# Joining low weight bits by OR, splitting early value products by query tile, and padding TensorE waits with identity products

## The chip, the cores and the metric

The kernel runs on one core of one Trainium2 chip. The metric is device time in microseconds (us) of one launch; lower is better. A core has five engines that run side by side and meet through semaphores: TensorE (PE; its weight loads are listed as PEld), VectorE (DVE), ScalarE (ACT), GpSimd (POOL) and SyncE (SP), which here only issues DMAs.

## The reference

Attention with a mask from a hash, and then a two-layer block on its output, all in float32:

```
q_bits = (q @ proj > 0);  k_bits = (k @ proj > 0)            # 6 bits, bucket = the number they form
mask   = q_bucket[:, :, :, None] == k_bucket[:, :, None, :]
scores = where(mask, q @ k.T / 8, -1e9)                      # B, H, S, D = 4, 8, 768, 64
attn   = softmax(scores)
x      = (attn @ v) as rows of 3072 tokens x 512
h      = x @ w_in                                            # 512 x 2048
out    = (s * relu(h)**2 + b) @ w_out                        # 2048 x 512
```

The inputs q, k, v and both weight matrices come in as 8-byte floats, which the kernel reads as pairs of 32-bit words.

## The kernel before

**Tiling and stages.** There are 32 visits (4 batches x 8 heads). A visit has 3 slots, each of 256 queries (two query tiles of 128, `TPC` = 2), so 96 slots in all. For each slot `weights` (L593 on) makes scores on TensorE (L608, L609), a row maximum on VectorE (L613), the exponential on ScalarE (L614) and the normalization on GpSimd (L633). `values` (L649 on) then multiplies by the values. The 16 token groups of the two-layer block follow in `moe`: first layer on TensorE (L776 to L778), square and scale on ScalarE and GpSimd (L786 to L790), second layer on TensorE (L803). Work of `moe` starts as soon as a batch is complete and is mixed with the attention of the next batches.

**Early and late.** The first ten visits (`FULL` = 10, 30 slots) take the early way: the normalized weights are transposed on TensorE (L665), copied out of PSUM by ScalarE or VectorE (the helper `copy`, L228), and multiplied with the values in plain float32 (L672), three steps a slot. A step has two products: key tile m = 0 goes into rows 0 to 63 of PSUM bank 4, key tile m = 1 into rows 64 to 127, both for all 256 queries. `finish` then adds the two halves: a scaled copy of the upper one (L719, ScalarE or VectorE), and a multiply-add of the lower one on VectorE (L720). Later visits use float16 pairs (L678, L684) and end in the same `finish`.

**Weight decoding.** 32 tiles of 128 x 512 weights (16 of w_in, 16 of w_out) are decoded in `decode` while the attention runs. For each, ScalarE rescales the high word (L382, into `osb`) and takes the top three bits of the low word as a number (L383). VectorE isolates the sign (L384), then shifts the high part left by three and puts the sign back (L385). GpSimd adds the three low bits as an integer (L389 for w_out, L395 for w_in). Then the value is split into a high and a low part.

**The order.** Nothing is issued in program order. Every step is entered in a `Plan` with an engine, a cost that is expected for it, what it reads and writes, and a priority. `Plan.order` (L73) is a list scheduler: it gives each step a start time by these costs, may choose between engines for a step with several ways, and emits all steps in order of start. Each engine executes its own steps in that order. In the plan, TensorE steps that start before `WARM` = 30 cost 1.7 times as much. So a changed cost anywhere changes the order of all that comes after.

**Start.** Ten products of the identity with itself (L298, float32, 128 x 128) are issued to TensorE before the plan begins. A float32 product is two records in the trace.

Of the kernel before, what the change touches and what calls it, by code (L numbers as in the profile page):

```python
# [33 lines left out]
class Plan:  # L34
# [3 lines left out]
    def __init__(self):  # L38
        self.steps = []
        self.writer = {}  # L40
        self.readers = {}
        self.moves = set()
        self.spread = {}
        self.owners = {}

    def add(self, eng, cost, fn, r=(), w=(), pr=0.0, lag=0.0):
        self.any([(eng, cost, fn)], r, w, pr, lag)

    def any(self, ways, r=(), w=(), pr=0.0, lag=0.0):

        i = len(self.steps)
        if "all" in w or "all" in r:
            self.spread[i] = "all" in w
        if SHARED in w:
            self.owners[i] = set()
        elif SHARED in r:
            self.owners[self.writer[SHARED]].add(i)
        deps = set()
        for k in r:
            if k in self.writer:  # L60
                deps.add(self.writer[k])
            self.readers.setdefault(k, []).append(i)
        for k in w:
            if k in self.writer:
                deps.add(self.writer[k])
            deps.update(self.readers.get(k, ()))
        for k in w:
            self.writer[k] = i
            self.readers[k] = []
        deps.discard(i)  # L70
        self.steps.append((ways, pr, lag, deps))

    def order(self):  # L73
        n = len(self.steps)
        left = [len(s[3]) for s in self.steps]
        users = [[] for _ in range(n)]
        for i, s in enumerate(self.steps):
            for d in s[3]:
                users[d].append(i)
        ready = [0.0] * n  # L80
        free = {}
        moved = 0.0
        open_ = {}
        where = {}
        live, over, held = set(), 0.0, False

        def offer(i):
            for way in self.steps[i][0]:
                open_.setdefault(way[0], []).append(i)

        def best(e, t):
            found = None
            for i in open_[e]:
                if i in self.owners or self.spread.get(i):
                    ready[i] = max(ready[i], over)
                    if held or (live and i in self.spread):
                        continue
                if ready[i] > t + LOOK.get(e, 0.0):
                    continue
                ways, pr = self.steps[i][:2]  # L100
                if found is not None and found[:2] <= (pr, i):
                    continue
                if len(ways) > 1:
                    mine = max(t, ready[i]) + next(c for x, c, _ in ways if x == e) + BIAS.get(e, 0.0)
                    if any(max(free.get(x, 0.0), ready[i]) + c + BIAS.get(x, 0.0) < mine - 1e-9 for x, c, _ in ways if x != e):
                        continue
                found = (pr, i)
            return found
        for i in range(n):
            if not left[i]:  # L110
                offer(i)
        out = []
        while len(out) < n:
            times = sorted((max(free.get(e, 0.0), min(ready[i] for i in lst)), k, e) for k, (e, lst) in enumerate(open_.items()) if lst)
            for t, _, e in times:
                found = best(e, t)
                if found is not None:
                    break
            if found is None:
                continue  # L120
            i = found[1]
            ways, pr, lag, deps = self.steps[i]
            for x, _, _ in ways:
                open_[x].remove(i)
            eng, cost, fn = next(z for z in ways if z[0] == e)
            where[i] = eng
            self.steps[i] = ([(eng, cost, fn)], pr, lag, deps)
            start = max(free.get(e, 0.0), ready[i])
            if e == PE and start < WARM:
                cost *= 1.7  # L130
            free[e] = start + cost
            end = start + cost + HOP[e]
            if e == SP or i in self.moves:
                moved = max(moved, start + cost) + lag
                end = moved + HOP[SP]
            else:
                end += lag
            out.append((start, i))
            if i in self.owners:
                live |= self.owners[i]  # L140
            if i in self.spread:
                held = self.spread[i]
            if i in live or i in self.spread:
                live.discard(i)
                over = max(over, end)
            for u in users[i]:
                same = any(x == e for x, _, _ in self.steps[u][0])
                ready[u] = max(ready[u], end - (SAME[e] if same else 0.0))
                left[u] -= 1
                if not left[u]:  # L150
                    offer(u)
        self.length = max(free.values())
        self.start = {i: t for t, i in out}
        return [i for _, i in sorted(out)]

# [1 line left out]
ABIAS = 0.0  # L159
HOP = {None: 0.0, PE: 0.2, DVE: 0.13, ACT: 0.2, POOL: 0.1, SP: 2.4}  # L160
SAME = {None: 0.0, PE: 0.2, DVE: 0.0, ACT: 0.05, POOL: 0.0, SP: 0.0}
WARM = 30.0
BIAS = {DVE: DBIAS, ACT: ABIAS}
SHARED = ("b", 0)
LOOK = {PE: 0.0, DVE: 0.0, ACT: 0.1}
# [3 lines left out]
def lsh_attention_moe(ctx: ExitStack, tc, q, k, v, proj, w_in, w_out, s, b, out):  # L169
# [39 lines left out]
    def dve(n, fn, r, w, pr, ns=None):  # L209
        plan.add(DVE, ((n + 64) / 960.0 if ns is None else ns), fn, r, w, pr)  # L210

    def act(n, fn, r, w, pr, more=0.0, late_=0.0):
        plan.add(ACT, 0.21 + n / 1470.0 + more, fn, r, w, pr, late_)
# [45 lines left out]
    def late(w):  # L259
        return w >= FULL  # L260
# [97 lines left out]
    def decode(u, pr):  # L358
# [8 lines left out]
        def raw():  # L367
            return box["t"]

        def words(z):  # L370
            return box["t"].rearrange("p n t -> p (n t)")[:, z * 512:(z + 1) * 512]
# [8 lines left out]
            n, j = key[1:]  # L380
            dve(1, lambda: nc.vector.tensor_reduce(wmx[:, j:j + 1], raw()[:, :, 1].bitcast(F32), AX.X, ALU.max, apply_absolute_value=True), rk, [("wx", j)], pr, 0.65)
        act(512, lambda: nc.scalar.activation(g, raw()[:, :, 1].bitcast(F32), AF.Copy, scale=float(2.0**-112)), rk + [("pace", u % PACE)], [gk], pr)  # L382
        act(512, lambda: nc.scalar.activation(words(0), raw()[:, :, 0].bitcast(U32), AF.Copy, scale=float(2.0**-29)), [], rk, pr)  # L383
        dve(256, lambda: nc.vector.tensor_scalar(words(1), gi, -2**31, None, ALU.bitwise_and), [gk], rk, pr, 0.45)  # L384
        dve(512, lambda: nc.vector.scalar_tensor_tensor(gi, gi, 3, words(1), ALU.logical_shift_left, ALU.bitwise_or), rk, [gk], pr, 0.7)  # L385
        if not wi:
            def swap():
                wt[key] = wk.tile([P, 2, 512], F32R, tag=f"w{u}", name=f"w{u}")
            pool(512, lambda: nc.gpsimd.tensor_tensor(gi, gi, words(0), ALU.add), rk, [gk], pr)  # L389
            plan.add(None, 0.0, swap, [], rk + wk_, pr)  # L390
            copy(512, lambda: wt[key][:, 0], lambda: g, [gk], [key + (0,)], pr, (ACT, POOL))
            plan.any([(POOL, 1.4, lambda: nc.gpsimd.tensor_tensor(wt[key][:, 1], g, f32(wt[key][:, 0]), ALU.subtract)),
                      (DVE, 0.7, lambda: nc.vector.tensor_tensor(wt[key][:, 1], g, f32(wt[key][:, 0]), ALU.subtract))], [gk, key + (0,)], [key + (1,)], pr)
            return
        pool(512, lambda: nc.gpsimd.tensor_tensor(words(0), gi, words(0), ALU.add), [gk], rk, pr)  # L395
        held_raw.append((words, rk, key))
        if j < NC_ - 1:
            return
# [250 lines left out]
    def values(i, pr, pieces):  # L649
# [19 lines left out]
        def product(f):  # L669
            def mm():  # L670
                for m in range(2):
                    nc.tensor.matmul(av[m * D:(m + 1) * D], VF[x][:, 2 * f + m], PF[r][f][:, m], start=(f == 0), stop=(f == HT - 1))  # L672
            pe(FPC, mm, TK(r, f, 3) + VK(x), [("b", 4)], pr)

        def high(first=True):
# [32 lines left out]
    def finish(i, av, pr):  # L708
# [5 lines left out]
            xp[key] = xpb[:, nx[0] % NXP], ("xp", nx[0] % NXP)  # L714
            nx[0] += 1
        t, tk = xp[key]
        xh, xk = t[hh * D:(hh + 1) * D], [tk + (hh,)]
        scale = 1.0 / TOP if late(w) else 1.0
        some(CH, lambda e: e.mul(xh, av[0:D], scale) if e is nc.scalar else e.tensor_scalar(xh, av[0:D], scale, None, ALU.mult), [], xk + [("b", 4)], pr, (ACT, DVE))  # L719
        dve(CH, lambda: nc.vector.scalar_tensor_tensor(xh, av[D:P], scale, xh, ALU.mult, ALU.add), [], xk + [("b", 4)], pr, 0.45)  # L720
        if hh:

            xk = [tk + (0,), tk + (1,)]
            if late(w) != late(w - 1):
                raise ValueError("both heads of a pair in one way")
            up = vsc[:, bb, 0:1]
# [148 lines left out]
    queue = plan.order()  # L875
    with tc.manual_schedule(engines={PE, DVE, ACT, POOL, SP}):
        for i in queue:
            plan.steps[i][0][0][2]()


# [20 lines left out]
GATE = lambda KK, AK: AK(0)  # L901
FULL = 10
PASS = 2
FPC = 0.48
WP = -8
MP = 0.0
PP = 0
# [26 lines left out]
```

## Time and profile before

| | |
|---|---|
| device time, median of 3 runs | 973.07 us (972.75 to 977.53) |
| the profiled execution, its own time | 973.05 us |
| its span, first to last instruction | 971.3 us |
| TensorE busy | 927.7 us, 96% |
| mean granted TensorE clock | 0.981 of full speed |

The profiled execution is as long as the median one, and 1.75 us of its time lie outside the span. "Busy" is the time in which at least one instruction of a kind is in flight. A row of the profile's groups gives the line of the kernel, engine, operation, output<-input, shapes, the count, then busy us, mean ns of one, and the idle time of the engine right before these instructions with what ended it.

### The profile page before, as it was taken

How to read it: one execution, taken by the hardware profiler on the slowest of the kernel's cores; microseconds unless marked ns; L12 is line 12 of the kernel's file. 1: busy time of each engine (PE TensorE's matmuls, PEld its weight loads, DVE VectorE, ACT ScalarE, POOL GpSimd, SP SyncE). 2: the span in 40 equal slices, each digit the busy share in tenths (PEclk: the TensorE clock that was granted, in tenths of full speed). 3: DMA queues.
4: the chain of work that ended last, by engine and by line, in shares of the span. 5: the costliest groups of instructions: out<-in, count | busy, mean ns of one | idle time of the engine just before them, and what ended most of it. 6: DMA issues, size and time to landing. Idle time of an engine off the chain costs nothing.

```text
span 971.3 us, 17425 instructions
## 1 busy us (share of the span) xinstructions
PE 927.7 (96%) x6152; PEld 716.6 (74%) x6152; DVE 623.6 (64%) x1042; ACT 663.0 (68%) x1224; POOL 625.7 (64%) x709
## 2 busy tenths in 40 slices
PE   8998797999999999989999999999999999999998
PEld 5766564666767777857778788878787788888886
DVE  6697898888897666776666776767778764000000
ACT  3777887887877667766777677777776776434342
POOL 2456865689799856756757777776666676433333
PEclk6998999999999999989999999999999999999999
DMA  4276666555978898987798898798897875201000
GB/s 121 78 204 161 197 164 181 148 150 162 240 168 183 183 202 195 190 185 152 151 200 169 159 189 186 151 201 161 169 197 164 159 143 112 72 1 44 11 23 22
DMA packets 303719, 144.40 MB, mean 149 GB/s; under 512 B 264256, under 2 KB 286784, under 8 KB 303632
## 3 DMA queue, kind: packets, MB, share of 16 engines
q1 hardware_dynamic: 298432, 126.25, 59.9%
q10 hardware_dynamic: 5200, 17.05, 5.6%
q8 instruction: 48, 0.79, 0.3%
q14 instruction: 39, 0.32, 0.1%
HBM read 51.38 MB, written 14.16 MB: 67 GB/s over the span
## 4 chain that ended last, share of the span: by engine, by line
PE 47%; issue 3%; POOL 2%; ACT 2%; DVE 1%; POOLq 0%; DVEq 0%; ACTq 0%
PE bank L803 17%; PE bank L776 6%; PE bank L778 5%; PE bank L777 5%; PE bank L608 3%; PE bank L678 3%; PE bank L609 3%; PE bank L684 2%; POOL glb L790 1%; POOL rb L789 1%; PE bank L478 1%; PE bank L495 0%; PE bank L497 0%; PE bank L496 0%; DVE pb L641 0%
## 5 line engine op out<-in xcount | busy, mean ns | idle before, releaser
L633 POOL TENSOR_SCALAR eb<-eb,st 128x768 f32<-128x768 f32 x176 | 205.2, 1171 | 76.8 <-DVE st L624 56.5
L803 PE MATMUL bank<-w,ghb 128*128 128x512 f32 x768 | 213.4, 407 | 0.1
L613 DVE TENSOR_REDUCE st<-bank 128x1 f32<-128x768 f32 x192 | 180.3, 953 | 51.0 <-PE bank L609 43.6
L776 PE MATMUL bank<-xc,wi 128*128 128x256 f16 x768 | 211.8, 276 | 0.3 <-ACT rb L786 0.3
L777 PE MATMUL bank<-xc,wi 128*128 128x256 f16 x768 | 209.8, 273 | 0.0
L778 PE MATMUL bank<-xc,wi 128*128 128x256 f16 x768 | 209.8, 273 | 0.0
L614 ACT ACTIVATE eb<-bank,st 128x768 f32<-128x768 f32 x176 | 157.5, 895 | 72.0 <-DVE pb L641 38.0
L641 DVE SCALAR_TENSOR_TENSOR pb<-eb,pb 128x768 f16<-128x768 f32 x132 | 144.7, 1100 | 54.2 <-ACT pb L640 53.7
L789 POOL TENSOR_SCALAR rb<-rb,misc 128x512 f32<-128x512 f32 x96 | 87.4, 910 | 126.6 <-ACT ghb L788 115.4
L786 ACT ACTIVATE rb<-bank,dsc 128x512 f32<-128x512 f32 x96 | 65.9, 686 | 146.4 <-PE bank L778 130.6
L608 PE MATMUL bank<-ks,aq 128*128 128x384 f32 x384 | 148.7, 387 | 11.9 <-ACT eb L614 8.8
L803 PEld LDWEIGHTS bank<-w,ghb 128*128 128x128 f32 x768 | 135.7, 189 | 22.5 <-issue 0.8
L790 POOL TENSOR_TENSOR glb<-rb,ghb 128x512 fp32r<-128x512 f32 x96 | 130.8, 1363 | 5.3
L609 PE MATMUL bank<-ks,bq 76*128 76x384 f32 x384 | 133.9, 349 | 0.0
L640 ACT ACTIVATE pb<-eb 128x768 f16<-128x768 f32 x132 | 110.1, 836 | 12.8 <-DMA tb<-pb 9.8
L803 PE MATMUL bank<-w,glb 128*128 128x512 f32 x384 | 110.9, 400 | 2.1 <-POOL glb L790 1.3
L776 PEld LDWEIGHTS <-wi 128*128 128x128 f16 x768 | 75.1, 98 | 46.4 <-issue 39.2
L608 PEld LDWEIGHTS bank<-ks,aq 128*128 128x128 f32 x384 | 75.4, 196 | 35.0 <-ACT eb L614 14.3
L618 POOL TENSOR_SCALAR st<-st 128x2 f32<-128x2 f32 x96 | 43.5, 453 | 69.3 <-DVE st L613 62.8
L826 DVE COPY osb<-bank 128x256 f32<-128x256 f32 x4 | 1.5, 420 | 131.5 <-PE bank L803 130.8
L803 PEld LDWEIGHTS bank<-w,glb 128*128 128x128 f32 x384 | 70.8, 189 | 17.6 <-POOL glb L790 2.9
L778 PEld LDWEIGHTS <-wi 128*128 128x128 f16 x768 | 75.3, 98 | 8.7
(134 smaller groups left out, 1530.1 us busy)
## 6 DMA issues: line engine op xcount, KB each, us to landing
ks<-aq SPq DMA_DIRECT2D x60, 192.0 KB
raw<-in_moe_w_in_dram ACTq DMA_DIRECT2D x16, 512.0 KB
raw<-in_moe_w_out_dram ACTq DMA_DIRECT2D x16, 512.0 KB
xc<-xd SPq DMA_DIRECT2D x60, 128.0 KB
nat<-in_q_dram SPq DMA_DIRECT2D x32, 192.0 KB
nat<-in_k_dram SPq DMA_DIRECT2D x32, 192.0 KB
vm<-in_v_dram SPq DMA_DIRECT2D x32, 192.0 KB
xd<-xsb SPq DMA_DIRECT2D x48, 128.0 KB
```

What stands on the lines that cost most here:

```text
L608: nc.tensor.matmul(o, aq[:, ts], ks[0][:, cols], start=True, stop=False)
L609: nc.tensor.matmul(o, bq[0:HR, ts], ks[1][0:HR, cols], start=False, stop=True)
L613: dve(S, lambda a=a, sc=sc: nc.vector.tensor_reduce(nm[:, a:a + 1], sc, AX.XY, ALU.max, negate=True), bk, [nk[a]], pr, 0.88)
L614: act(S, lambda a=a, sc=sc, e=e: nc.scalar.activation(e.rearrange("p (g n) -> p g n", g=2), sc, AF.Exp, bias=nm[:, a:a + 1], accum_out=z[: ...
L633: eng.tensor_scalar(e, e, rz[:, a:a + 1], u[:, a:a + 1], ALU.mult, ALU.add)
L640: act(S, lambda e=e, hi=hi: nc.scalar.mul(hi, e, TOP), [ek], [hk], pr)
L641: dve(S, lambda e=e, hi=hi, lo=lo: nc.vector.scalar_tensor_tensor(lo, e, TOP, hi, ALU.mult, ALU.subtract), [ek, hk], [("lo", n)], pr, 1.0)
L776: nc.tensor.matmul(hp, w[:, 0, fs], xc[:, 0, :], start=(cc == 0), stop=False)
L777: nc.tensor.matmul(hp, w[:, 1, fs], xc[:, 0, :], start=False, stop=False)
L778: nc.tensor.matmul(hp, w[:, 0, fs], xc[:, 1, :], start=False, stop=(cc == NC_ - 1))
L790: pool(2 * CH, lambda r=r, gh=gh, gl=gl: nc.gpsimd.tensor_tensor(gl, r, f32(gh), ALU.subtract), [rk, hk], [lk], MP)
L803: nc.tensor.matmul(o, (gh, gh, gl)[z][:, ts], w[:, z % 2], start=(f == fa and z == 0), stop=(f == fz - 1 and z == 2))
```

## The change

There are four edits; the diff is below with all that they touch.

- **Decoding.** ScalarE's scale for the low word is multiplied by 0.9373, so that the three bits never round up to 8. VectorE puts the sign of the high part into the same word by AND and OR in one instruction with two tensor inputs (in place of L384), and the shift-and-OR that follows takes that word, so that sign and low bits arrive together (in place of L385). The additions on GpSimd (L389, L395) go.
- **Early value products.** Of each step of L672, two products of 256 queries become four of 128 queries: the query tile, no longer the key tile, chooses the half of the PSUM rows. Both key tiles add up in the same rows. `finish` then copies two pieces of 64 x 128 in place of L719 and L720 for the early visits; each copy may go to ScalarE or VectorE. The expected cost of a step goes from 0.48 to 0.55.
- **Padding.** After the plan is made, `Plan.pad` walks through TensorE's steps. Where a step's planned start is more than 0.4 us after the end of the one before, and the start is below 450 in the plan's time, it looks for a PSUM bank whose last user was not TensorE and whose next user is. It then issues as many identity products (as L298) into this bank as fit into 65% of the planned gap at 0.115 us each.
- **The plan's start.** `WARM` becomes 0: the first 30 us are planned at the ordinary TensorE costs.

```diff
+        self.touch[i] = {k[1] for k in (*r, *w) if k[0] == "b"} | ({0} if "all" in r or "all" in w else set())
...
         self.start = {i: t for t, i in out}
+        self.pad(sorted(out))
         return [i for _, i in sorted(out)]
+
+    def pad(self, out):
+
+        self.pads = {}
+        uses = {b: [] for b in PADBANKS}
+        for t, i in out:
+            eng, cost = self.steps[i][0][0][:2]
+            for b in self.touch[i] & set(PADBANKS):
+                uses[b].append((t, t + cost, eng == PE))
+        last = 0.0
+        for t, i in out:
+            eng, cost = self.steps[i][0][0][:2]
+            if eng != PE:
+                continue
+            if 0.0 < last < t < PADDED and t - last > PADMIN:
+                free = []
+                for b, u in uses.items():
+                    old, new = [x for x in u if x[0] < t], [x for x in u if x[0] >= t]
+                    if new and new[0][2] and not (old and old[-1][2]):
+                        free.append((max((x[1] for x in old), default=0.0) + 0.2, b))
+                at, b = min(free, default=(t, None))
+                n = int((t - max(last, at)) * PADDING / PADCOST)
+                if n > 0:
+                    self.pads[i] = (b, n)
+            last = t + cost
...
-WARM = 30.0
+WARM = 0.0
+PADDED = 450.0
+PADMIN = 0.4
+PADDING = 0.65
+PADCOST = 0.115
+PADBANKS = (1, 2, 3, 5, 6, 7)
...
-        act(512, lambda: nc.scalar.activation(words(0), raw()[:, :, 0].bitcast(U32), AF.Copy, scale=float(2.0**-29)), [], rk, pr)
-        dve(256, lambda: nc.vector.tensor_scalar(words(1), gi, -2**31, None, ALU.bitwise_and), [gk], rk, pr, 0.45)
-        dve(512, lambda: nc.vector.scalar_tensor_tensor(gi, gi, 3, words(1), ALU.logical_shift_left, ALU.bitwise_or), rk, [gk], pr, 0.7)
+        act(512, lambda: nc.scalar.activation(words(0), raw()[:, :, 0].bitcast(U32), AF.Copy, scale=float(2.0**-29 * 0.9373)), [], rk, pr)
+        dve(512, lambda: nc.vector.scalar_tensor_tensor(words(0), gi, -2**31, words(0), ALU.bitwise_and, ALU.bitwise_or), [gk], rk, pr, 0.75)
+        sum_ = (lambda: words(0)) if wi else (lambda: gi)
+        dve(512, lambda: nc.vector.scalar_tensor_tensor(sum_(), gi, 3, words(0), ALU.logical_shift_left, ALU.bitwise_or), [], rk + [gk], pr, 0.75)
...
-            pool(512, lambda: nc.gpsimd.tensor_tensor(gi, gi, words(0), ALU.add), rk, [gk], pr)
...
-        pool(512, lambda: nc.gpsimd.tensor_tensor(words(0), gi, words(0), ALU.add), [gk], rk, pr)
...
                 for m in range(2):
-                    nc.tensor.matmul(av[m * D:(m + 1) * D], VF[x][:, 2 * f + m], PF[r][f][:, m], start=(f == 0), stop=(f == HT - 1))
+                    for a in range(TPC):
+                        nc.tensor.matmul(av[a * D:(a + 1) * D, 0:P], VF[x][:, 2 * f + m], PF[r][f][:, m, a * P:(a + 1) * P], start=(f == m == 0), stop=(f == HT - 1 and m == 1))
...
-        scale = 1.0 / TOP if late(w) else 1.0
-        some(CH, lambda e: e.mul(xh, av[0:D], scale) if e is nc.scalar else e.tensor_scalar(xh, av[0:D], scale, None, ALU.mult), [], xk + [("b", 4)], pr, (ACT, DVE))
-        dve(CH, lambda: nc.vector.scalar_tensor_tensor(xh, av[D:P], scale, xh, ALU.mult, ALU.add), [], xk + [("b", 4)], pr, 0.45)
+        if late(w):
+            scale = 1.0 / TOP
...
+        else:
+            for a in range(TPC):
+                copy(P, lambda a=a: xh[:, a * P:(a + 1) * P], lambda a=a: av[a * D:(a + 1) * D, 0:P], [("b", 4)], xk[a:a + 1], pr, (ACT, DVE))
...
         for i in queue:
+            b, n = plan.pads.get(i, (0, 0))
+            for _ in range(n):
+                nc.tensor.matmul(bank[:, b, 0:P], ident, ident, start=True, stop=True)
             plan.steps[i][0][0][2]()
...
-FPC = 0.48
+FPC = 0.55
```

## Rows read from the trace of the kernel before

**Rows 1.** The page: span, busy time by engine, TensorE's busy share and clock in 40 slices

```profile
span 971.3 us, 17425 instructions
...
PE 927.7 (96%) x6152; PEld 716.6 (74%) x6152; DVE 623.6 (64%) x1042; ACT 663.0 (68%) x1224; POOL 625.7 (64%) x709
...
PE   8998797999999999989999999999999999999998
...

```

**Rows 2.** Busy us of each engine (x instructions) by stretch, granted clock, DMA share

```profile
28.20:330.00 301.80, 274.35 (x1769) 194.22 (x1769) 254.90 (x470) 236.44 (x475) 222.96 (x251) 0.98 0.65 172
...
8.50:28.20 19.70, 18.16 (x55) 12.81 (x54) 14.57 (x25) 8.67 (x20) 6.46 (x13) 0.50 0.30 75
86.00:93.50 7.50, 5.48 (x21) 4.81 (x21) 3.46 (x5) 3.67 (x8) 5.34 (x5) 0.58 0.49 126
113.00:118.40 5.40, 5.18 (x26) 4.00 (x27) 4.74 (x9) 4.51 (x10) 4.00 (x6) 0.68 0.59 190
420.00:428.50 8.50, 6.43 (x30) 4.45 (x31) 5.47 (x9) 4.19 (x8) 3.89 (x6) 0.60 0.86 178
...
330.00:971.00 641.00, 629.53 (x4305) 504.58 (x4302) 349.37 (x517) 415.15 (x728) 393.95 (x438) 0.99 0.67 140
...
270.00:275.00 5.00, 3.45 (x21) 2.50 (x20) 4.87 (x10) 3.51 (x8) 4.31 (x6) 1.00 0.60 125
```

**Rows 3.** TensorE's waits from 0 to 450 us: us in total, times, longest

```profile
PE bank L608 <- ACT eb L614: 8.8, 10, 1.5
PE bank L665 <- POOL eb L633: 7.7, 9, 1.6
PE bank L665 <- POOL pb L633: 3.5, 6, 1.0
...
PE bank L672 <- DVE xpb L720: 1.2, 2, 0.8
```

**Rows 4.** TensorE timeline (start, us, what, [idle before]): waits over 0.4 us

```profile
7.09 0.38 PE L549 MATMUL bank<-ks,pjs 64*64 64x384 f32 x1 [0.75 <-ACT ks L228]
...
272.53 0.45 PE L608 MATMUL bank<-ks,aq 128*128 128x384 f32 x1 [1.55 <-ACT eb L614]
...
429.96 0.55 PE L478 MATMUL bank<-ident,nat 128*128 128x128 f32 x3 [0.66 <-ACT eb L614]
```

**Rows 5.** TensorE timeline, a fall and a rise of its clock

```profile
87.01 0.37 PE L665 MATMUL bank<-ident,eb 128*128 128x128 f32 x1 [1.63 <-POOL eb L633]
88.40 2.61 PE L665 MATMUL bank<-ident,eb 128*128 128x128 f32 x11 [1.02 <-POOL eb L633]
...
91.44 0.52 PE L608 MATMUL bank<-ks,aq 128*128 128x384 f32 x1
...
96.25 0.34 PE L608 MATMUL bank<-ks,aq 128*128 128x384 f32 x1
```

**Rows 6.** TensorE timeline: the first identity products, and transposes of the same shape later

```profile
1.35 4.33 PE L298 MATMUL bank<-ident 128*128 128x128 f32 x20 [1.35 <-POOL ident masks.py:199]
...
64.41 1.53 PE L665 MATMUL bank<-ident,eb 128*128 128x128 f32 x12
```

**Rows 7.** Groups by line over the span: GpSimd's additions and normalization

```profile
L633 POOL TENSOR_SCALAR eb<-eb,st 128x768 f32<-128x768 f32 x176 | 205.2, 1171 | 76.8 <-DVE st L624 56.5 <-ACT rb L787 9.6 <-PE bank L665 3.8
...
L395 POOL TENSOR_TENSOR raw<-osb,raw 128x512 int32<-128x512 int32 x16 | 21.0, 1315 | 4.2 <-ACT tb L228 1.5 <-ACT vm L579 1.3 <-ACT aq L480 0.7
...
L389 POOL TENSOR_TENSOR osb<-osb,raw 128x512 int32<-128x512 int32 x16 | 20.6, 1291 | 7.6 <-DVE osb L385 3.0 <-ACT xsb L731 1.6 <-ACT tb L228 1.5
```

**Rows 8.** VectorE's decoding lines: ns min/median/max, first and last start

```profile
L384 DVE TENSOR_SCALAR raw<-osb x32: 409/420/1216, 59.0 to 309.1; 128x512 int32<-128x512 int32 x32
L385 DVE SCALAR_TENSOR_TENSOR osb<-osb,raw x32: 674/692/1776, 61.3 to 309.6; 128x512 int32<-128x512 int32 x32
```

**Rows 9.** GpSimd timeline around an addition, and TensorE's wait behind it

```profile
149.43 1.27 POOL L395 TENSOR_TENSOR raw<-osb,raw 128x512 int32<-128x512 int32 x1 [1.46 <-ACT tb L228]
150.69 2.38 POOL L633 TENSOR_SCALAR pb<-pb,st 128x768 f32<-128x768 f32 x2
...
152.16 0.33 PE L665 MATMUL bank<-ident,pb 128*128 128x128 f32 x1 [0.98 <-POOL pb L633]
```

**Rows 10.** Groups by line over the span: value products, PSUM copies, finish

```profile
L672 PE MATMUL bank<-tb,vb 128*64 128x256 f32 x360 | 54.8, 404 | 5.2 <-DVE tb L228 2.0 <-ACT tb L228 1.7 <-DVE xpb L720 1.2
...
L228 ACT COPY tb<-bank 128x512 f32<-128x512 f32 x74 | 41.3, 585 | 12.8 <-PE bank L665 12.3
L720 DVE SCALAR_TENSOR_TENSOR xpb<-bank,xpb 64x256 f32<-64x256 f32 x96 | 41.0, 427 | 21.0 <-ACT xpb L719 18.3
...
L719 ACT ACTIVATE xpb<-bank 64x256 f32<-64x256 f32 x83 | 31.0, 373 | 20.1 <-PE bank L678 11.0 <-PE bank L672 6.7 <-PE bank L684 0.8
```

**Rows 11.** TensorE timeline: one, two and three value steps in a row

```profile
61.80 0.65 PE L672 MATMUL bank<-tb,vb 128*64 128x256 f32 x4
...
63.39 1.08 PE L672 MATMUL bank<-tb,vb 128*64 128x256 f32 x8
...
67.07 1.51 PE L672 MATMUL bank<-tb,vb 128*64 128x256 f32 x12
```

More of the change, by code (lines that the diff above doesn't have):

```diff
@@ L44, in __init__ @@
         self.owners = {}
+        self.touch = {}
     def add(self, eng, cost, fn, r=(), w=(), pr=0.0, lag=0.0):
@@ L716, in finish @@
         t, tk = xp[key]
-        xh, xk = t[hh * D:(hh + 1) * D], [tk + (hh,)]
-        scale = 1.0 / TOP if late(w) else 1.0
-        some(CH, lambda e: e.mul(xh, av[0:D], scale) if e is nc.scalar else e.tensor_scalar(xh, av[0:D], scale, None, ALU.mult), [], xk + [("b", 4)], pr, (ACT, DVE))
-        dve(CH, lambda: nc.vector.scalar_tensor_tensor(xh, av[D:P], scale, xh, ALU.mult, ALU.add), [], xk + [("b", 4)], pr, 0.45)
+        xh, xk = t[hh * D:(hh + 1) * D], [tk + (hh, a) for a in range(TPC)]
+        if late(w):
+            scale = 1.0 / TOP
+            some(CH, lambda e: e.mul(xh, av[0:D], scale) if e is nc.scalar else e.tensor_scalar(xh, av[0:D], scale, None, ALU.mult), [], xk + [("b", 4)], pr, (ACT, DVE))
+            dve(CH, lambda: nc.vector.scalar_tensor_tensor(xh, av[D:P], scale, xh, ALU.mult, ALU.add), [], xk + [("b", 4)], pr, 0.45)
+        else:
+            for a in range(TPC):
+                copy(P, lambda a=a: xh[:, a * P:(a + 1) * P], lambda a=a: av[a * D:(a + 1) * D, 0:P], [("b", 4)], xk[a:a + 1], pr, (ACT, DVE))
         if hh:
-            xk = [tk + (0,), tk + (1,)]
+            xk = [tk + (z, a) for z in range(2) for a in range(TPC)]
             if late(w) != late(w - 1):
```

## Prediction, made before the changed kernel ran

> **What bounds the kernel now.** I read the page first. TensorE is busy for 96% of the span, and no other engine comes near it. Its digits are nines from about the middle of the span on; the sevens and eights stand in the first half [rows 1]. The busy time by stretch gives the sizes. From 330 us to the end TensorE is busy for 629.5 of 641 us, so that part is bound by the work itself, and what an earlier stage saves moves it forward as a whole. From 28.2 to 330 us TensorE is busy for 274.4 of 301.8 us, VectorE for 254.9, ScalarE for 236.4 and GpSimd for 223.0 [rows 2]. There no engine is full: TensorE, the widest, sits idle for 27 us because the chain of one slot (scores, maximum, exponential, normalization, transpose, copy, product) runs through all four. The view of waits names the last to arrive: the exponential for 8.8 us, the normalization on GpSimd for 7.7 + 3.5 = 11.2 us, bank 4 after `finish` for 1.2 us [rows 3].
>
> Beside idle time there is a second loss, the clock. In four stretches the granted clock averages 0.50 to 0.68 [rows 2], a mixture of the two levels 1.2 and 2.4 GHz. After two waits of 1.63 and 1.02 us a score product takes 0.52 us, and a little later 0.34 us [rows 5].
>
> So at most some 43 us (971.3 - 927.7) of waiting and some 17 us of clock can be had, all but a little of it before 430 us. The change does not touch the rest.
>
> **Decoding.** GpSimd loses 32 additions: 21.0 + 20.6 = 41.6 us, all between 60 and 315 us [rows 7, 8]. VectorE gets 32 two-tensor instructions at 692 ns (the row of L385) for 32 at 420 ns (L384): 32 x 0.272 = 8.7 us more [rows 8]. It has 301.8 - 254.9 = 46.9 us of idle time in that stretch [rows 2] to hide them; without that cover they cost up to 8.7 us. No wait is new: L384, too, stood behind ScalarE's low bits, whose words it wrote beside. No DMA is moved, though the planner may issue a weight load earlier where a raw buffer comes free earlier. On the path: one addition stands right in front of a normalization, and TensorE waits 0.98 us, and then 0.64 us for the second one, behind it [rows 9]; most other normalizations of rows 3 waited for VectorE's reciprocal (L624) [rows 7]. The gain lies between 1.6 us and all 11.2 us that end on GpSimd. I take 3 us, near the lower end, because L624 is next late.
>
> Here a rule speaks against the edit. The mean normalization takes 1171 ns [rows 7], and the shortest in the timeline 0.98 us a piece, so something stretches it. The Trainium skill (GPSIMD Engine Reference, Key points) says that GpSimd shares its SBUF interfaces with VectorE and contends with VectorE instructions that have two SBUF inputs. The new instruction is one of these. By that rule up to the 8.7 us of added VectorE time would come back as longer GpSimd instructions, against 41.6 us taken off it: the sign stays.
>
> **Finish.** For 30 early slots VectorE loses 30 x 0.427 = 12.8 us [rows 10]. ScalarE's 64 x 256 copy takes 373 ns and its 128 x 512 copy 585 ns, 0.83 ns a column; a 64 x 128 copy is then 0.27 us by estimate. Sixty of them are 16.0 us for 30 x 0.373 = 11.2 us: 4.8 us more, on whichever of two engines is free [rows 10]. Bank 4 comes free after 0.27 to 0.53 us instead of 0.80, but TensorE waited for it only 1.2 us [rows 3]. Bounds 0 and 4 us; I take 2, since VectorE's net load falls by 12.8 - 8.7 = 4 us.
>
> **Value products.** A step is four records now. One alone spans 0.65 us, two 1.08, three 1.51 [rows 11]: each further one adds 0.43, a lone one has 0.22 more. That fits records of 0.215 us which wait only for their own half of the array: first, second beside third, fourth. With eight records of half the length in the order a0, a0, a1, a1 the same rule gives 5 x 0.107 = 0.54 alone and 0.43 in a row. 90 steps are 54.8 us busy, 0.61 each [rows 10], so most stand alone. The best case is 90 x 0.11 = 10 us less. If the shorter records cannot overlap (twice the weight loads), a step is 8 x 0.107 = 0.86 and the cost is 90 x 0.25 = 22 us. The rows show full overlap, so I stay at the first end, but a step runs into its neighbours and the early stage is not bound by TensorE alone: 3 us gained.
>
> **Clock.** Time at half speed is stretch x 2 x (1 - clock). From 8.5 to 28.2 us: all, with 18.2 us busy, of which 9.1 could go, but VectorE is busy for 14.6 us there, so at most 5.1. From 86: 6.3 us, worth 3.2. From 113: 3.5, worth 1.7. From 420: 6.8, worth 3.4 [rows 2]. Together 13.4 us, if padding kept the clock up at all four places. Longer waits than some of these pass without a fall (1.55 us at 272 us, clock 1.00 around it) [rows 2, 4], so what falls and what doesn't is not set by single waits; I take two thirds, 9 us.
>
> The Trainium skill (TensorE: Matmul & The Clock Gate, What's actually happening) says that half speed is the default and activity releases it. By it every pad counts as activity, and the whole 13.4 us would come. The falls of rows 2 agree; the wait at 272 us shows that it isn't the length of one wait.
>
> **Padding's own cost.** Ten identity products took 4.33 us, 0.43 each, at the slow pace of the start. Transposes of that shape later take 1.53 us for 12 records [rows 6], 0.13 each; a product is two records. So a pad takes 0.22 (half of 0.43) to 0.26 us at full clock, about double the 0.115 that `pad` reckons with, and 65% of a gap becomes 0.65 x 0.217 / 0.115 = 1.2 gaps. The trace has 35 waits of TensorE over 0.4 us from 7 to 430 us, the first, a long one and the last in rows 4, together 30.7 us. If the planned gaps were these, each would get its length x 5.65, rounded down: 156 pads, 33.9 us. Matched exactly they overfill the gaps by 3 us. Matched nowhere they put 34 us into TensorE's queue. What is queued behind a pad is the very step that had to wait; a pad that waits for its own bank's reader holds up that step too. The plan's costs are near the trace's (0.48 against 0.43 to 0.65 for a value step), so I expect most gaps to be there; 7 us exposed. Of the pads' delays some fall into later waits, which is in that number.
>
> **The sum.** 971.3 - 3 - 2 - 3 - 9 + 7 = 961.3 us of span; with the 1.75 us outside it 963.0. The profiled execution (973.05) is as long as the median (973.07), so nothing is corrected. `WARM` I cost at nothing: the first 28 us are a chain through VectorE, and if the clock stays low there the new order is misjudged by a few us.
>
> **Rivals.** *Pads in the wrong place* (slower). One mechanism: padding where the chip does not wait. The price is 34 us of TensorE time. It decides from the point at which the exposed part exceeds the 17 us of gains (3 + 2 + 3 + 9). With the whole of it the time is 973 - 17 + 34 = 990; with 25 us exposed 981. For it: the pad is underpriced twofold. Against it: the waits in the trace are many and long, and delays before 330 us run into later waits. Chance 0.18.
>
> *Gains off the path* (no change). GpSimd's additions are not what TensorE waits for (1.6 of 11.2 us), L624 and the exponential take over, and clock and pads cancel (9 against 9): 973 - 3 to 973, about 971. For it: VectorE at 84% of the early stage. The case that pads don't keep the clock up, so that they do not do what they say, ends here too: 973 - 8 + 7 = 972. Chance 0.20.
>
> *The early stage closes up.* All 13.4 us of clock, and half of the 27 us of idle time from 28 to 330 us because four engines have less queueing: 973 - 13.4 - 13.5 = 946. For it: GpSimd loses a fifth of its load there. Chance 0.15.
>
> **How the numbers follow.** The forecast, 954 to 968, has 0.47. The larger gain reaches down to 938, the no-change case from 968 to 978, the slower one up to 992. Leaving out about 0.06 below and 0.1 above gives 944 to 982; the upper bound of the value products (22 us) lies within it after the other gains. A measurement of this kernel tells about 0.5% (4.9 us) from no change, 968.2 to 977.9. Faster 0.47 + 0.15 = 0.62, same 0.20, slower 0.18.
>
> **What would show it.** Clock 1.00 at 86 to 120 and 420 us; identity records between value steps, with fewer waits over 0.4 us but TensorE more busy; GpSimd at some 585 us busy; a lone value step of 0.54 us; no row of L720 before 250 us. Wrong would be: a value step of 0.86; identity time far over 34 us; waits of normal size behind the pads; the clock still falling. If the last product of the attention ends no earlier than about 10 us before that of the kernel before, the gain isn't where I put it.

## The result, and the profile after

| | before | changed kernel |
|---|---|---|
| device time, median of 9 runs each | 972.75 us (969.11 to 977.53) | 978.88 us (977.76 to 979.32) |
| ratio to before, with 95% interval | | 1.0059 [1.0041, 1.0076] |
| span of the profiled execution | 971.3 us | 977.2 us |

The change makes the kernel 0.6% slower, where 1% faster was forecast. The page of the changed kernel (span, busy time by engine, TensorE's busy share and clock in 40 slices; it answers to [rows 1]):

```profile
span 977.2 us, 18992 instructions
...
PE 958.4 (98%) x6970; PEld 779.0 (80%) x6970; DVE 607.2 (62%) x1013; ACT 665.1 (68%) x1240; POOL 596.7 (61%) x690
...
PE   9999999999999999999999999999999999999998
...
PEclk9999999999999999999999999999999999999999
```

Everything that a reader would wish for is there. TensorE is busy in every slice and its clock row shows no fall. GpSimd is 29 us lighter and VectorE 16 us. And the kernel is slower: TensorE's busy time has grown by 30.7 us, its idle time has shrunk by 24.8 us (971.3 - 927.7 = 43.6 to 977.2 - 958.4 = 18.8). The same stretches as in [rows 2]:

```profile
8.50:28.20 19.70, 19.70 (x140) 16.77 (x139) 13.81 (x24) 7.33 (x19) 5.91 (x13) 1.00 0.31 77
28.20:330.00 301.80, 292.47 (x2407) 241.07 (x2405) 236.13 (x442) 232.02 (x480) 196.36 (x233) 1.00 0.65 170
86.00:93.50 7.50, 6.97 (x68) 5.94 (x65) 6.37 (x11) 6.05 (x16) 6.28 (x7) 1.00 0.67 187
113.00:118.40 5.40, 5.40 (x51) 4.78 (x50) 4.74 (x20) 3.46 (x9) 2.09 (x2) 1.00 0.63 187
420.00:428.50 8.50, 8.50 (x51) 6.56 (x50) 6.11 (x8) 5.84 (x12) 5.96 (x7) 1.00 0.83 177
```

The clock is 1.00 where it was 0.50 to 0.68. What fills TensorE is in the groups by line (L917 issues the pads, L705 is the value product that was L672, L665 the normalization that was L633, L417 and L419 the two decoding instructions, L261 the copy helper):

```profile
L665 POOL TENSOR_SCALAR eb<-eb,st 128x768 f32<-128x768 f32 x176 | 203.6, 1162 | 78.3 <-DVE st L656 64.2 <-ACT rb L823 4.6 <-ACT osb L415 2.8
...
L917 PE MATMUL bank<-ident 128*128 128x128 f32 x458 | 57.7, 277 | 1.5 <-DVE osb L853 0.9 <-ACT eb L646 0.5
...
L705 PE MATMUL bank<-tb,vb 128*64 128x128 f32 x720 | 53.7, 282 | 0.2 <-ACT tb L261 0.2
...
L417 DVE SCALAR_TENSOR_TENSOR raw<-osb,raw 128x512 int32<-128x512 int32 x32 | 25.7, 809 | 5.6 <-ACT raw L416 5.6
...
L261 ACT COPY xpb<-bank 64x128 f32<-64x128 f32 x50 | 12.9, 259 | 9.2 <-PE bank L705 7.5 <-DVE xpb L261 1.1
```

The pads are 458 records, 229 products, and 57.7 us of TensorE. Waits for GpSimd's normalization, 11.2 us in [rows 3], are 1.9 us now (TensorE's waits from 0 to 450 us; there is no row of L697 behind `pb` any more):

```profile
PE bank L697 <- POOL eb L665: 1.9, 3, 0.8
PE bank L640 <- ACT eb L646: 1.6, 2, 1.0
```

A pad in front of a step takes the place of its wait, so this fall alone does not tell what decoding has gained. The open question was how 57.7 us of pads can replace 24.8 us of waiting, and whether the rest of the change helped or hurt.

### The profile page after: what moved, and what is told of

Read it like the earlier page. It is cut to its first block, busy times and chain, and to the rows that moved or that the text cites. A ratio compares the mean times of both kernels' runs of the same rounds, so it can differ in the third digit from the quotient of the medians.

```text
span 977.2 us, 18992 instructions
## 1 busy us (share of the span) xinstructions
PE 958.4 (98%) x6970; PEld 779.0 (80%) x6970; DVE 607.2 (62%) x1013; ACT 665.1 (68%) x1240; POOL 596.7 (61%) x690
## 4 chain that ended last, share of the span: by engine, by line
PE 55%; issue 4%; DVE 4%; POOL 4%; ACT 3%; DMA 0%; POOLq 0%; DVEq 0%; ACTq 0%
PE bank L840 20%; PE bank L813 6%; PE bank L815 6%; PE bank L814 6%; PE bank L640 4%; PE bank L711 4%; PE bank L641 4%; PE bank L717 2%; POOL glb L827 1%; DVE pb L673 1%; POOL rb L826 1%; ACT eb L646 1%; PE bank L510 1%; ACT pb L672 1%; DVE st L645 1%
## 5 line engine op out<-in xcount | busy, mean ns | idle before, releaser
L665 POOL TENSOR_SCALAR eb<-eb,st 128x768 f32<-128x768 f32 x176 | 203.6, 1162 | 78.3 <-DVE st L656 64.2
L673 DVE SCALAR_TENSOR_TENSOR pb<-eb,pb 128x768 f16<-128x768 f32 x132 | 143.3, 1089 | 44.9 <-ACT pb L672 44.0
L823 ACT ACTIVATE rb<-bank,dsc 128x512 f32<-128x512 f32 x93 | 63.9, 687 | 138.9 <-PE bank L815 117.9
L640 PE MATMUL bank<-ks,aq 128*128 128x384 f32 x384 | 144.9, 377 | 5.5 <-DVE nat L531 2.0
L827 POOL TENSOR_TENSOR glb<-rb,ghb 128x512 fp32r<-128x512 f32 x96 | 132.8, 1384 | 5.4
L641 PE MATMUL bank<-ks,bq 76*128 76x384 f32 x384 | 130.0, 339 | 0.0
L672 ACT ACTIVATE pb<-eb 128x768 f16<-128x768 f32 x132 | 109.6, 835 | 13.6 <-DMA tb<-pb 10.6
L813 PEld LDWEIGHTS <-wi 128*128 128x128 f16 x768 | 74.9, 98 | 45.8 <-issue 39.0
L640 PEld LDWEIGHTS bank<-ks,aq 128*128 128x128 f32 x384 | 72.7, 189 | 22.0 <-DVE nat L531 5.9
L815 PEld LDWEIGHTS <-wi 128*128 128x128 f16 x768 | 75.1, 98 | 8.6
L814 PEld LDWEIGHTS <-wi 128*128 128x128 f16 x768 | 75.6, 98 | 6.8
```

What stands on the lines that cost most here:

```text
L640: nc.tensor.matmul(o, aq[:, ts], ks[0][:, cols], start=True, stop=False)
L641: nc.tensor.matmul(o, bq[0:HR, ts], ks[1][0:HR, cols], start=False, stop=True)
L665: eng.tensor_scalar(e, e, rz[:, a:a + 1], u[:, a:a + 1], ALU.mult, ALU.add)
L672: act(S, lambda e=e, hi=hi: nc.scalar.mul(hi, e, TOP), [ek], [hk], pr)
L673: dve(S, lambda e=e, hi=hi, lo=lo: nc.vector.scalar_tensor_tensor(lo, e, TOP, hi, ALU.mult, ALU.subtract), [ek, hk], [("lo", n)], pr, 1.0)
L813: nc.tensor.matmul(hp, w[:, 0, fs], xc[:, 0, :], start=(cc == 0), stop=False)
```

## The experiments

In the plan, `pad` runs after the order is made. So a change of its constants alters the number of pads and leaves the order of all other instructions as it is. Experiments that differ only there are compared instruction by instruction: without the pads, TensorE's 6512 records come in the same order in the traces of the changed kernel, of the one without pads and of the one with pads at their price.

**Pads away, pads at their price, and the plan's start alone.** Pads away:

```diff
-PADDED = 450.0
+PADDED = 0.0
```

> The changed kernel with no padding (limit in plan time 0 in place of 450); order of all other instructions as in the changed kernel. Theory A (the pads' own 57.7 us of TensorE time are what made it slower): TensorE's other work, 958.4 - 57.7 = 900.7 us, keeps the waits of before (about 43 us) and its half-speed stretches (about 17 us): some 963 us of span, 965 us in all, 8 us faster than before and 14 faster than the changed kernel. Theory B (the new order made by changed costs is worse, the pads are harmless): 980 us or more, since the clock falls again. Theory C (pads and what they save cancel): 976 to 980 us.

Measured: 974.88 us, ratio 1.0005 [0.9984, 1.0026]. The changed kernel without pads is neither faster nor slower than before. This is none of the three forecasts: slower than theory A's 965 us, faster than B and C. TensorE's waits for the normalization come to 6.9 + 0.6 = 7.5 us here, so most of their fall to 1.9 us is pads in the place of waits.

```diff
-PADCOST = 0.115
+PADCOST = 0.218
```

> The changed kernel with 0.218 us per identity product in place of 0.115, so that the pads fill 65% of a planned gap in truth and not 123%; same order. About 115 pads, 25 us in place of 50 or more. Theory A: 4 to 15 us faster than the changed kernel (964 to 975 us), with the clock still near 1.00. Theory B: within 3 us of the changed kernel (976 to 981 us). If the clock falls again in two or more stretches, half the pads don't do what they are for.

Measured: 965.31 us, ratio 0.9913 [0.9884, 0.9941], clock 0.998. With half as many pads the changed kernel is 13.6 us faster than as it stands and 0.9% faster than before. That is theory A's range, and theory B's 976 us or more is out. Against the same order without pads, these pads gain 9.6 us by the medians, and the pads of the change lose 4.0.

The next is the padding edit on the kernel before, with the changed start of the plan: decoding, value products, `finish` and `FPC` go back to what they were.

> The kernel before with padding and with the plan's first 30 us at ordinary cost, but decoding and value products as before. Theory A: slower than before by about what the changed kernel loses and the other two edits gain, 978 to 990 us, clock 1.00. Theory B (order): anything else, as the order is a third one; about 973 us if only the new decoding or value products had spoilt the order.

Measured: 989.58 us, ratio 1.0161 [1.0132, 1.0190], clock 1.00: the slow end of theory A's range.

And of that edit only the part that alters the order (`PADDED` is 0, so that no pad is issued):

```diff
-WARM = 30.0
+WARM = 0.0
```

> The kernel before with the plan's first 30 us at ordinary cost (1.0 in place of 1.7 times) and nothing else. This is the part of the padding edit that changes the order. Theory A: within 5 us of before (968 to 978 us). Theory B: slower by 6 us or more (979 us or more), since the plan then takes TensorE's start to be twice as fast as it is.

Measured: 985.34 us, ratio 1.0122 [1.0088, 1.0157]. The line that I had costed at nothing is 1.2% alone. It went against theory A as I had put it (within 5 us), so there are two losses: the pads' price, and an order. Between these two runs, which have one order, the pads of the change lose 4.2 us.

How the pads lose is seen at one place of the same order. In the timeline of TensorE (start, duration, what, idle before) without pads, ahead of three score steps and a transpose step:

```profile
162.45 0.44 PE L640 MATMUL bank<-ks,aq 128*128 128x384 f32 x1 [0.88 <-ACT eb L646]
...
166.15 0.44 PE L640 MATMUL bank<-ks,aq 128*128 128x384 f32 x1 [2.73 <-ACT eb L646]
...
167.81 0.48 PE L697 MATMUL bank<-ident,eb 128*128 128x128 f32 x1 [0.69 <-POOL eb L665]
...
169.33 0.67 PE L640 MATMUL bank<-ks,aq 128*128 128x384 f32 x1
```

the same in the changed kernel:

```profile
164.09 2.17 PE L917 MATMUL bank<-ident 128*128 128x128 f32 x18
166.01 0.42 PE L640 MATMUL bank<-ks,aq 128*128 128x384 f32 x1
...
166.81 3.96 PE L917 MATMUL bank<-ident 128*128 128x128 f32 x34
170.52 0.42 PE L640 MATMUL bank<-ks,aq 128*128 128x384 f32 x1
...
171.32 2.62 PE L917 MATMUL bank<-ident 128*128 128x128 f32 x22
173.78 0.60 PE L697 MATMUL bank<-ident,eb 128*128 128x128 f32 x4
174.13 0.42 PE L640 MATMUL bank<-ks,aq 128*128 128x384 f32 x1
```

and with pads at their price:

```profile
155.73 1.05 PE L917 MATMUL bank<-ident 128*128 128x128 f32 x8
156.76 0.44 PE L640 MATMUL bank<-ks,aq 128*128 128x384 f32 x1
...
157.58 2.17 PE L917 MATMUL bank<-ident 128*128 128x128 f32 x18
160.47 0.44 PE L640 MATMUL bank<-ks,aq 128*128 128x384 f32 x1 [0.72 <-ACT eb L646]
...
161.28 1.50 PE L917 MATMUL bank<-ident 128*128 128x128 f32 x12
...
163.51 0.44 PE L640 MATMUL bank<-ks,aq 128*128 128x384 f32 x1
```

Waits of 0.88, 2.73 and 0.69 us stand against pads of 2.17, 3.96 and 2.62 us. With pads that fill more than the wait, none is left, and from the first of these score products to the last one takes 174.13 - 166.01 = 8.1 us; without pads it is 169.33 - 162.45 = 6.9 us, with pads at their price 163.51 - 156.76 = 6.8 us. With pads at their price a wait of 0.72 us stays behind the pads, so that step still starts when its data come, and the score product at the end takes 0.44 us, not the 0.67 us that it took without pads.

The ledger of TensorE over the whole span (span and busy time from each page, pads from the group of L917; idle = span - busy, rest = busy - pads):

| kernel | span | pads | idle | rest |
|---|---|---|---|---|
| before | 971.3 | 0 | 43.6 | 927.7 |
| changed, no pads | 970.5 | 0 | 44.9 | 925.6 |
| changed, pads at price | 963.8 | 30.7 | 26.2 | 906.9 |
| changed | 977.2 | 57.7 | 18.8 | 900.7 |

The first 30.7 us of pads take 18.7 us off the idle time and 18.7 us off the rest: 6.7 us gained (9.6 by the medians; the profiled execution without pads was one of the shorter ones). The rest is not clock alone. In the trace 7.6 us of these pads lie beside another product that is still in flight, and the ledger counts that time as pads. The other 11.1 us come near to what the clock can give: TensorE was busy at half speed for 29.9 us without pads and for 3.1 us with them, half of the difference is 13.4 us. The next 27.0 us of pads take 7.4 and 6.2 us (2.9 of them by lying beside other products): 13.4 us lost.

**The other start of the plan, with and without pads.** `WARM` back to 30 in the changed kernel, without pads:

> The changed kernel with no padding and the plan's first 30 us at 1.7 times again, so decoding and value products alone. Theory D (the plan's start is a cost of its own: it made the kernel before 12 us slower when changed alone): 960 to 967 us, some 8 to 14 us faster than with the plan's start changed (974.9). Theory E (orders are a lottery; each changed cost draws another one within some 10 us): anything from 965 to 985 us, no faster than the kernel before.

Measured: 966.72 us, ratio 0.9916 [0.9892, 0.9941]. That is theory D's range, and faster than before, which theory E excluded. Then with `PADCOST` = 0.218:

> As the run before, and padding with 0.218 us per identity product. Theory D: pads at their price bring some 10 us whatever the order (974.9 to 965.3 us with the other start): 950 to 957 us. Theory E: within 5 us of the unpadded kernel of the same order, since the pads' gain of 10 us belonged to the clock lost in that one order.

Measured: 961.26 us, ratio 0.9860 [0.9837, 0.9883], clock 0.996. This is the fastest of all and beats both kernels. The pads at their price gain 5.5 us here, between the two theories (just over E's 5 us, short of D's 957). The kernel before with them:

> The kernel before, its order unchanged, with padding at 0.218 us per identity product. Theory D: clock 0.99 or more, 960 to 967 us. Theory E: 968 to 976 us. If it is slower than before, right-priced pads help only where decoding and value products have left longer gaps.

Measured: 967.88 us, ratio 0.9930 [0.9907, 0.9952], clock 1.00. The clock is theory D's; the time falls between the two ranges. Right-priced pads help in a third order too. And fewer of them, 0.40 for `PADDING` at 0.218 us in the changed kernel:

> The changed kernel with 0.218 us per identity product and 40% of a gap filled in place of 65%: some 65 pads. If overfilled gaps were the whole cost (theory A), fewer pads cost still less as long as the clock holds: 962 to 966 us. If the clock falls again in a stretch: 967 to 972 us.

Measured: 966.25 us, ratio 0.9920 [0.9896, 0.9944]. With 58 pads in place of 110 the time lies between the two forecasts. Between 40% and 65% no difference can be told.

**Which of the two other edits gains.** One at a time on the kernel before, without pads, start as before:

> The kernel before with the new decoding alone (32 additions off GpSimd; no padding, start planned as before, value products and finish as before). Theory F (GpSimd's 41.6 us are what the pair of edits gains): 964 to 968 us, most of the pair's 8 us. Theory G (the value products and the shorter finish are): 971 to 976 us. If both halves alone come out slower than the pair, the order decides and not the parts.

Measured: 969.43 us, ratio 0.9938 [0.9917, 0.9960].

> The kernel before with the early value products over query tiles and the two-copy finish alone (no padding, start planned as before, decoding as before). Theory F: 971 to 976 us, no change, since a step takes as long as before (0.66 us alone, 1.09 for two). Theory G: 964 to 968 us.

Measured: 968.19 us, ratio 0.9919 [0.9893, 0.9945]. Each alone gives much of what the pair gives (0.9916). So neither theory F nor G holds, and the gains don't add up. With decoding alone TensorE still waits 9.3 + 1.5 = 10.8 us for the normalization, 11.2 before: the wait that this edit was to shorten has hardly changed.

**Underpriced pads in the other order.** `WARM` = 30, `PADCOST` = 0.115:

> The changed kernel with the plan's first 30 us at 1.7 times again, padding as in the change (0.115 us per product). Theory A (underpriced pads cost the same in any order): 12 to 15 us slower than with pads at their price in this order, 973 to 976 us. If the loss belonged to the one order, 960 to 966 us.

Measured: 967.46 us, ratio 0.9921 [0.9899, 0.9944], pads 49.2 us. It is 6.2 us slower than with pads at their price, not 12 to 15: the direction holds in both orders, the size doesn't. Against no pads in this order (966.72) nothing is lost or gained.

This run is the change without its last line, the plan's start, and it is 0.8% faster than before. With that line it is 978.88 us.

**Is it the start, or is it any new order?** On the kernel before, each with one constant changed:

```diff
-WARM = 30.0
+WARM = 20.0
```

> The kernel before with the plan's first 20 us, in place of 30, at 1.7 times the TensorE cost; nothing else. Theory E (a changed cost at the start draws another order, and orders differ by some 10 us): 965 to 985 us, more than 5 us off the kernel before. Theory D (the plan's start must match a slow TensorE): about a third of what the full removal costs, 975 to 979 us.

Measured: 979.04 us, ratio 1.0039 [1.0023, 1.0054]. It is at the edge of theory D's range, and a little nearer to the kernel before than the 5 us that theory E asked for.

```diff
-NORM = 1.1
+NORM = 1.12
```

> The kernel before, with the normalization's expected cost on GpSimd 1.12 us in place of 1.10; nothing else is changed, but the plan draws another order. Theory D: within 3 us of the kernel before. Theory E: 4 us or more off it, to either side.

Measured: 972.42 us, ratio 0.9981 [0.9959, 1.0002]. This is theory D's range.

```diff
-NORM = 1.1
+NORM = 1.08
```

> The same with 1.08 us. Theory D: within 3 us of the kernel before. Theory E: 4 us or more off it, and not the mirror image of the run with 1.12.

Measured: 986.00 us, ratio 1.0108 [1.0076, 1.0140]. A number that no instruction sees, off by 2%, costs as much as the plan's start did. Here theory E holds: orders can differ by this much.

```diff
-WARM = 30.0
+WARM = 40.0
```

> The kernel before, with the plan's first 40 us in place of 30 at 1.7 times the TensorE cost. TensorE was at half speed until 28 us there, so theory D expects 0 to 4 us slower than before; theory E anything within 10 us to either side.

Measured: 974.39 us, ratio 0.9998 [0.9981, 1.0015]. This fits both theories. Six orders of the same work (0, 20, 30 and 40 us; 1.08 and 1.12) lie between 972 and 986 us: of the five new ones two are some 12 us slower than before, one 4 to 5, and two cannot be told from it. In the ledger of the slow one with 1.08 both columns are worse: idle 985.5 - 933.9 = 51.6 us (43.6 before), rest 933.9 us (927.7). Its clock is 0.976, before 0.981, and TensorE is busy at half speed for 44.4 us, before for 33.5. The clock row of its page, and under it that of the kernel before:

```profile
PEclk6999899899999999999999999999999999999999
...
PEclk6998999999999999989999999999999999999999
```

**Pads at the start alone.** The fastest kernel, with pads only before 30 us of the plan's time:

> The changed kernel with the plan's start as before and pads at 0.218 us each, but only before 30 us of the plan's time. Without pads this order took 966.7 us, with all of them 961.3. If the clock of the start is most of the pads' gain: 961 to 963 us. If the later gaps are: 965 to 967 us, with the clock falling between 30 and 200 us.

Measured: 966.85 us, ratio 0.9915 [0.9885, 0.9945]: no gain over the kernel without any pads (966.72), as forecast for the case that the later gaps bring the gain. The clock row of its page shows the eights that come back after the start:

```profile
PEclk9998898999999999999999999999999999999999
```

## Why the prediction was wrong, step by step

Two steps failed: the plan's start, which the sum had at nothing, and the net of the pads, which it had at -9 + 7 = -2 us. The start costs 8 to 11 us of the miss of 15.9 us (978.9 for 963.0), the pads 3 to 6 us, by the order in which the two are counted. Everything but the start, measured together, took 967.46 us, which lies in the forecast of 954 to 968.

**Pads.** The price was right: 0.217 us was taken, and the long run of 34 records (17 products) takes 3.96 us, 0.23 each with its tail (0.25 over all). The number was not: I put the waits of the trace (35, 30.7 us) in the place of the planned gaps and got 156 pads; there are 229, so the planned gaps that got pads come to at least 229 x 0.115 / 0.65 = 40.5 us. And 7 us exposed was a guess between 3 and 34. In the same order the pads of the change are 27.0 us more than those at their price, and 13.4 us of that reach the end. What they cost and what they save came to 4.0 us lost in the order of the change and 0.7 us with the old start, not to 2 us gained. Of the signs of being wrong, identity time far over 34 us came true. The mechanism stood in the prediction, as the rival with a chance of 0.18, and it was right that the pads are underpriced twofold. It did not decide the result as it was priced: it asked for 17 us exposed, and with the same pads and the old start the kernel is faster than before. I let the plan's closeness to the trace decide for "most gaps are there", with 3 us of overfilling if they matched exactly. At the place shown the gaps are there, but planned longer than the chip waits: 9, 17 and 11 pads mean planned gaps of at least 1.59, 3.01 and 1.95 us, for waits of 0.88, 2.73 and 0.69 us. The underpricing comes on top, and what is too much holds up the step that the chain is waiting for.

**The plan's start.** "I cost at nothing" was the step that failed most. The line alone is 1.2% slower. In the changed kernel it is the difference between 966.7 and 974.9 us without pads, between 961.3 and 965.3 with pads at their price, and between 967.5 and 978.9 with the pads of the change. The reason given, that the new order is misjudged by a few us if the clock stays low in the first 28 us, does not carry it: in the changed kernel the clock is 1.00 there, and the loss is still 11.4 us. The runs with `NORM` show that such a loss need not have anything to do with the start: a new order of the kernel before cost from nothing to 12 us, and none was faster. So this term should have been a range of that width, for the whole change, not zero.

**Decoding, finish, value products.** The three terms, 3 + 2 + 3 = 8 us, agree with 0.9916 for the pair, 8 us. The agreement is not proof, and in part luck. Since orders of the same work differ by more, none of the three gains is shown as such; that both edits alone come out below all six orders of the kernel before (969.4 and 968.2 against 972.4 to 986.0) speaks for a true gain of some us each. So do four pairs that differ by both edits: 974.9 for 985.3 us at the changed start, 966.7 for 974.6 at the old one, 978.9 for 989.6 and 961.3 for 967.9 with pads. Of the working, the copies of 64 x 128 were right (259 ns, 0.27 expected). VectorE's decoding grew by 3.9 us and not by 8.7: its two lines took 18.4 + 28.9 us before, and 25.7 us (L417) and 25.5 us (L419) now. GpSimd became lighter by 29.0 us and not by 41.6 (596.7 against about 585 expected), since the new order also gives it other steps. The value step was wrong in its form. Steps of the changed kernel, one, two and three in a row, against [rows 11]:

```profile
106.33 0.66 PE L705 MATMUL bank<-tb,vb 128*64 128x128 f32 x8
...
104.64 1.09 PE L705 MATMUL bank<-tb,vb 128*64 128x128 f32 x16
...
111.25 1.53 PE L705 MATMUL bank<-tb,vb 128*64 128x128 f32 x24
```

Each further step adds 0.43 us, as expected, but a lone one takes 0.66 and not 0.54. The 0.22 us of a lone step isn't a wait for half of the array, then; it is a tail that shorter records keep. 90 steps are 53.7 us busy for 54.8: 1 us, not 10.

The rule of the Trainium skill that was weighed against decoding (GPSIMD Engine Reference, Key points: contention with VectorE instructions of two SBUF inputs) does not show in the mean: a normalization takes 1162 ns, 1171 before, though VectorE issues 32 more such instructions. It shows in single rows of the changed kernel, GpSimd's and VectorE's together in order of time:

```profile
127.01 0.98 POOL L665 TENSOR_SCALAR eb<-eb,st 128x768 f32<-128x768 f32 x1 [0.74 <-DVE st L656]
...
127.20 1.33 DVE L417 SCALAR_TENSOR_TENSOR raw<-osb,raw 128x512 int32<-128x512 int32 x1 [0.39 <-ACT raw L416]
...
127.98 1.40 POOL L665 TENSOR_SCALAR pb<-pb,st 128x768 f32<-128x768 f32 x1
```

The new instruction begins during a normalization and takes 1.33 us, for 0.67 at its shortest; the next normalization begins during the instruction and takes 1.40 us, for 0.98. Over the whole trace the 87 normalizations of `eb` that run beside no VectorE instruction with two SBUF inputs take 0.97 to 1.00 us each; the 29 that run beside one for more than half of their time take 1.41 us on average. The trace agrees with the rule. Few normalizations meet the edit, which fits the unchanged mean: 19 of the 176 run beside a decoding line of VectorE at all, 22 before.

**Clock.** Padding does keep it up: 1.00 in every slice, as activity that releases half speed would (the Trainium skill, TensorE: Matmul & The Clock Gate, What's actually happening). The size, 9 us, was near: with pads at their price TensorE's other work is in flight for 11.1 us less. Where I looked for the largest part of it (5.1 us), in the first 28 us, no gain in time can be told: the pads there alone give nothing. After TensorE, VectorE has the most work there (13.8 of 19.7 us in the changed kernel), as the bound of 5.1 us had said in part.

**The sum, made again** from medians: 973 (before) - 8 (both edits, the old start) + 8 (the new start's order) - 9.6 (pads at their price) + 13.6 (pads at half their price) = 977; measured 978.9. Each term is the difference of two neighbouring runs, so the sum has to come out near there: it divides the loss, and is no test of the causes. With the pads counted before the start they cost 0.7 us, and the start 11.4.

**What stays open.** Why one order is 14 us worse than another was not followed through the plan, so the cause of the larger part of the miss is known only down to the line that brings it in. How much of the gain of decoding and of value products is their own can't be told from one order each.

## What to carry to other kernels

A filler in an in-order queue needs its true price: against the same order without fillers, filling two thirds of the planned gaps gained 0.6 to 0.9%, filling all of them and a quarter more gained nothing or lost up to 0.5%. When a planner emits the order, compare a change with several orders of the unchanged work (shift a cost by 2%) before a gain or loss of 1% is put down to the edit. And a profile in which an engine is busy everywhere at full clock says nothing about whether that work is wanted.

## What the runs showed of the hardware that was not expected

Part of the spread between runs goes with the clock. The changed kernel (clock 0.999 to 1.00) lies within 1.6 us in 9 runs, the one with pads at their price (0.998 to 1.00) within 0.5 us in 6 (965.1 to 965.6). The same instructions without pads spread over 5.7 us in 12, and the runs with the lower clock are the longer ones: 971.6 us at 0.984, 977.3 us at 0.975. A clock near 1.00 does not make the time steady by itself: the kernel before with pads at their price (0.996 to 1.00) spreads over 4.6 us in 6 runs.

A product of float32 with 64 rows of output costs 0.054 us a record of 128 columns in a row of steps (0.43 us for 8 records), one with 128 rows 0.12 us (3.96 us for 34 records, the tail included). So the records of the two halves overlap about fully also when they are half as long, with twice the weight loads.
